# A fused attention and spectral filter kernel: two more key blocks moved off ScalarE, another closing sequence, and a new order of issue

## The chip, the cores and the metric

The kernel runs on one core of a Trainium2 chip. A core has five engines that work side by side and meet at semaphores: TensorE (matrix products, in the profile PE, its weight loads PEld), VectorE (DVE), ScalarE (ACT), GpSimd (POOL) and SyncE (SP), which here issues DMA transfers only. The working memory SBUF and the accumulators' memory PSUM have 128 partitions; TensorE writes only to PSUM, in banks of 512 float32 columns per partition. The metric is device time in microseconds; lower is better. The profile shows one execution, whose span runs from its first to its last instruction.

## The reference

Two branches over the same kind of input, mixed by a gate for each token. Branch A is multi-head attention over 2048 tokens with 16 heads of width 28. Branch B multiplies the two-dimensional Fourier transform of its input by a complex weight. (In this case both inputs are the same array, and the kernel reads it once.)

```python
g = sigmoid((x * gate_w).sum(-1, keepdims=True))      # x: 1 x 2048 x 448
qkv = (x @ wqkv) -> q, k, v of 16 heads, 28 wide
p = softmax(q @ k^T * 28**-0.5)                        # 16 x 2048 x 2048
a = (p @ v) @ wo
b = irfft2(rfft2(x) * (w_r + 1j * w_i))
return g * a + (1 - g) * b
```

## The kernel before

**Attention.** The heads are taken in four groups of four, the queries in four chunks of 512, so there are 16 rounds (group, chunk). A round goes over 16 key blocks of 128 keys. A unit is one head's product of a key block with a query chunk, 128 x 512 scores. Four heads lie in four row strips of TensorE, so that single scores of different heads can run beside each other. Per round and key block there is also a value product (`pv`): four column strips at once, the exponentials times the values, accumulated over all the round's blocks in one PSUM bank `pvb`. One more column of the values holds the weights alone, so that the bank also gets the softmax's denominators.

The exponential of a unit is taken in one of two ways, by key block:

- On ScalarE. Units follow each other in steps of three and two. A step's scores go to the PSUM slot `psA` (three banks) or `psB` (two banks), one ScalarE instruction (line 956) takes the exponentials of the whole slot into a ring in SBUF, and one value product per key block reads them.
- Off ScalarE. `ND` says how many of a round's blocks, counted from the last, go this way: 55 of 256. Each of the four units is one single score (`dunit`) into one of the two shared PSUM banks `bg`; VectorE adds an offset and writes the result as a 16-bit integer (`conv`, line 991), whose bits are read as a bfloat16 power of two with a linear mantissa. Three copies with integer offsets (`phase`, line 1002, 32, 64 and 96 steps) shift the mantissa's error, and four value products with scaled values `vd` add the four versions up, so that the errors average out. A block costs no ScalarE time, but four single scores, four conversions, three phase shifts and four value products instead of one. A phase shift runs on GpSimd, unless its number is in the list that ends `PLAN`; then it runs on VectorE (81 of 165).

**After a round** (`normalise`) VectorE copies the bank to SBUF (line 1070), a DMA gathers the denominators, VectorE takes the reciprocals, GpSimd multiplies them by the gate, two DMA stages spread them over the partitions (`Rb`), and GpSimd multiplies (line 1081). The last round (`last_norm`, from line 1091) does it without DMA: VectorE turns the bank in 32 x 32 blocks, takes reciprocals, multiplies by the gate, multiplies the values and turns back, all in two halves of 256 columns, one after the other.

**Branch B** is a chain of products with constant matrices through the same two `bg` banks, each evacuated by VectorE, with DMA regroupings between the stages.

**Output.** `out_tile` computes one of 16 blocks of 128 tokens by 448 in eight products: four for branch B, four for the four head groups. Blocks 12 to 15 need the last round: their eighth product is `late`. Blocks 12 and 13 are gathered in `bg` banks, 14 and 15 in the first banks of `psA` and `psB`, which are free behind the last exponentials. ScalarE copies three of them to SBUF and VectorE copies block 14, and the stores go out by SP (12, 14) and ScalarE's queue (13, 15).

**The gate** (`gate_item`, from line 876): ScalarE takes an exponential of 16 columns, four small VectorE operations (lines 880 to 885) follow, and a small product turns the result.

**The order.** Each of some 2,950 operations is recorded with its engine, inputs and a rough duration; a planner outside the kernel has put them in one order, packed as text in `PLAN` with the bank numbers and the list of phase shifts on VectorE. `issue` emits them in that order; an engine executes its own in order, so an instruction that waits holds up all behind it on its engine. `issue` adds one more kind of wait: when an operation of VectorE is marked `lk`, the next GpSimd operation in the order waits for it.

Of the kernel before, what the change touches and what calls it, by code (L numbers as in the profile page):

```python
# [16 lines left out]
ACT = mybir.ActivationFunctionType  # L17
# [14 lines left out]
ND = [0,3,3,4,4,4,4,4,4,4,4,4,4,4,3,2]  # L32
# [11 lines left out]
        'c-j@#V;dMovw-2*nOV$kY}>YN+qP}nwv#rt*@kUw+qRvw&3Vtq=MUW1gJ1x_LUa%yhy)5^fQQHsASOfshFA~*G(?5i&<)~14RBBi'  # L44
        '>Ox$o3H6{B#Dn?}A1Xp^XaEVI5j2N{&=@K}3upp~pd}=RrqBwKKpW@?Nue!7gig>7l0kdl8QMc~=mOE8gHH*mAT^|gjy?sXfnLxZ'
        'GD2lY2bmx}^oCBp2V{WE(AoEao{$ClLO<x@v%+A=26>^Y&ki|Y1muKVPznb7{E!dELT<<d1)wUFhS^XM3PDMj1BGEA6oF(o4$43Z'
        'Ope2#EX;*@P!x(mH7E}Ap#+qJ1+WmRz#=FQzrhwriCdw+p9H_dHrNiSaEPA_J0K0F#>FteFM*}74937)cn8a2pnnf(@dH$c6_5@;'
        '!W77WBOyJmgnoW1OoLT05vIcocrF<+6V8I2&>wceA21XCgrSfbv*2zR<WIvHI18&`5S)W-I0V+fdB}<vU;tc%OK=(1!82J8S0FoX'
        'fC;b>a^NV~40~Wa?1fFR4|3vg*bljIG#r3Dm>aLcUqJS6=nB{1Ivj+&cmvqpghP-I55rfu1^MwC+=c@93BJP}_yKjGAQr-(&;dTf'
        '7buKHup!)qW^fda!EyKpPQX1Vip6j(oPt$+AC7>rC!sZHyPAvR8ZLoZ{94ZHv-#}4B$mPzoWpw?>`ML@N@E%P4}JkCrBIc{a!BeC'  # L50
        'Jcjc41Xw+VbzA`-zzeW8f?dxQ@g-Eki1s;b=E_(FpTQ>H!ezX(Wqmnc-dDwHSiwiODb)t9j@!8grcyh2Bd1o8Y#LP)YhhZomBnu3'
        'sJ1pnvkze>*TE=u7r&HOQWxvtZceAttLQd^s*i8rwKTvOHlckZe{e?C5Z_88%xE*IM7A+D!9AQq?d6>6HRMvcRa0z+e{&v{)&9we'
        '?LlsiEpQ)au=_c)%A(TQn6@Rh!dGyBv#P&1n`(`1FuOX<hdI4H!%1yhJkISfi9Nxer9F1QBb>t~vtPujL+n&XJjq|B6N);;US+eL'
        'F{q>51#{YC96?1?U9lUU<47v98m_uy6x9PqsF5nAJ<Fq1Pwa)G)ius!d*gM!!hJA{y~=~sc^<4%*}iy*`{59EnTM+6wm)XJ!_);H'
        'fGO-nPHhL`AiTj*RdzcVhu|1BR*h5R)h!;1!!VkfprWgr977Gqv^J)?%Ofz2y~nZCNF0T^tX8pA9A#8=jH^cD7>uXxa}E1|AM#in'
        'hmZI+SFv|^Jig)y_?oNPr(DENR536nPQ*zV3n!`A7zc~m$ru+a*(V$ir(kg#Ulp@&cq&fA$*Q`2%a3`AnvNxGe4MIY@C>YK6X8pK'
        '#tCpH&cf%M1WVc?J|TYO+4zCy;3uwVYuVbisGp1Tu$X_(-=w&oj|=b}m+;@^ha^x5)lW&J7UClOM-r>jHi`NT|Ks1Wl>NoURZW{$'
# [160 lines left out]
class Op:  # L218
    def __init__(self, eng, dur, emit, deps, key, **a):
# [18 lines left out]
        self.id = None  # L238


class Item:
# [1113 lines left out]
```

## Time and profile before

| | |
|---|---|
| time, median of 3 runs | 393.71 us (393.5 to 394.0) |
| profiled execution, own time | 393.18 us |
| its span | 391.4 us |
| instructions | 11986 |
| PE busy | 375.8 us (96%) |
| ACT busy | 373.7 us (95%) |
| DVE busy | 325.6 us (83%) |
| POOL busy | 226.9 us (58%) |
| granted TensorE clock | 1.000 |

Busy time is the time in which at least one record of an engine runs. The records of ScalarE's and TensorE's neighbours overlap, so their pace is read from the distance of their starts. In a row of the view by order of time stand start, duration, engine, line, operation, output and inputs, shapes and, in brackets, the idle time before it with what ended it. In a row of the view by groups stand the count, the busy time, the mean duration in ns of one, and the group's idle time with what ended it. All matrix products carry the line of the helper that records them (415 or 423), so they are told apart by their tiles: `psA<-q,k` and `psB<-q,k` are scores for ScalarE, `bg<-q,k` single scores, `pvb<-ring,vw` and `pvb<-pd,vd` value products, `bg<-wo,q` and `bg<-Bd,X` output products.

### The profile page before, as it was taken

To read this page: it belongs to the slowest core of one execution; us is meant where nothing else is said; L and a number is where in the kernel's file an instruction comes from. 1 tells how busy PE (TensorE), PEld (TensorE's weight loads), DVE (VectorE), ACT (ScalarE), POOL (GpSimd) and SP (SyncE) were. 2 spreads that over 40 slices of the span, in tenths; PEclk is the share of its full clock that TensorE was granted. 3 is DMA by queue.
4 is the path that set the end of the run, shared out by engine and by line. 5 is a ranking of instruction groups with operands and counts; after the bars stand their busy time and mean duration, and the time that the engine had idled before them with its cause. 6 is when DMAs were issued, how large, how long until landed. Compare 5 with 4: busy or idle time off the path is not lost.

```text
span 391.4 us, 11986 instructions
## 1 busy us (share of the span) xinstructions
PE 375.8 (96%) x4926; PEld 139.0 (36%) x4926; DVE 325.6 (83%) x530; ACT 373.7 (95%) x340; POOL 226.9 (58%) x234
## 2 busy tenths in 40 slices
PE   8999999899999999999999999999999999999996
PEld 5643323234433334433333334422223332333332
DVE  2778777978799999999999999999999977977123
ACT  4999999899999999899999999999999999999993
POOL 7033777343965489868567786774655884524200
PEclk9999999999999999999999999999999999999999
DMA  8730000011202112222234122211012121010111
GB/s 208 175 107 3 3 13 2 4 17 32 88 10 67 42 28 72 65 74 58 49 91 130 27 66 66 66 39 39 3 38 93 61 72 43 22 62 26 53 37 60
DMA packets 31954, 21.64 MB, mean 55 GB/s; under 512 B 16716, under 2 KB 29740, under 8 KB 31900
## 3 DMA queue, kind: packets, MB, share of 16 engines
q1 hardware_dynamic: 30540, 20.43, 19.5%
q8 instruction: 38, 0.62, 0.6%
q10 hardware_dynamic: 1360, 0.46, 0.5%
q14 instruction: 16, 0.13, 0.1%
HBM read 15.00 MB, written 1.97 MB: 43 GB/s over the span
## 4 chain that ended last, share of the span: by engine, by line
PE 60%; DVE 19%; ACT 11%; issue 4%; DMA 3%; SPq 1%; POOL 1%; DVEq 0%; POOLq 0%; ACTq 0%
PE bg L415 28%; PE pvb L415 18%; ACT ring L956 10%; DVE pd L991 8%; PE psA L415 7%; PE psB L415 6%; DVE pd L1002 3%; DMA xtok<-in_A_x_dram 3%; SPq L398 1%; DVE tt L1244 1%; POOL pd L1002 1%; DVE pvs L1070 1%; PE bg L423 1%; DVE X L1193 1%; DVE k L721 1%
## 5 line engine op out<-in xcount | busy, mean ns | idle before, releaser
L956 ACT ACTIVATE ring<-psA 128x1536 bf16<-128x1536 f32 x157 | 233.5, 1487 | 2.6 <-PE psA L415 1.7
L1002 POOL TENSOR_SCALAR pd<-pd 128x2048 uint16<-128x2048 uint16 x84 | 159.3, 1903 | 61.5 <-DVE pd L1002 34.9
L956 ACT ACTIVATE ring<-psB 128x1024 bf16<-128x1024 f32 (+1 forms) x157 | 166.2, 1059 | 2.6 <-PE psB L415 2.5
L991 DVE TENSOR_SCALAR pd<-bg 128x512 uint16<-128x512 f32 x220 | 145.0, 683 | 12.6 <-PE bg L415 5.6
L415 PE MATMUL bg<-q,k 32*128 32x512 bf16 x220 | 81.1, 379 | 4.7 <-DVE pd L991 2.9
L415 PE MATMUL pvb<-pd,vd 128*32 128x512 bf16 x880 | 79.7, 384 | 0.7 <-DVE pd L1002 0.3
L415 PEld LDWEIGHTS <-k 32*128 32x128 bf16 x1024 | 37.0, 91 | 110.7 <-issue 105.8
L415 PE MATMUL pvb<-ring,vw 128*32 128x512 bf16 x784 | 74.0, 384 | 0.3 <-DVE pvs L1070 0.2
L415 PE MATMUL psA<-q,k 32*128 32x512 bf16 x483 | 65.0, 383 | 0.5 <-ACT ring L956 0.3
L415 PE MATMUL psB<-q,k 32*128 32x512 bf16 x321 | 64.1, 383 | 0.4 <-ACT pd L956 0.2
L1002 DVE TENSOR_SCALAR pd<-pd 128x2048 uint16<-128x2048 uint16 x81 | 58.2, 733 | 0.8
L415 PEld LDWEIGHTS <-vd 128*32 128x32 bf16 x880 | 21.1, 94 | 38.6 <-issue 33.9
L1081 POOL TENSOR_TENSOR q<-pvs,Rb 128x512 bf16<-128x512 f32 x15 | 19.1, 1271 | 24.9 <-DMA Rb<-rsc 21.0
L415 PEld LDWEIGHTS <-vw 128*32 128x32 bf16 x804 | 20.0, 95 | 30.1 <-issue 25.7
L415 PEld LDWEIGHTS <-xT 112*128 112x128 bf16 (+1 forms) x512 | 19.6, 97 | 10.9 <-issue 7.5
L1150 DVE CAST fin<-bg 128x448 bf16<-128x448 f32 x12 | 7.5, 622 | 19.2 <-PE bg L415 19.1
L869 POOL TENSOR_TENSOR vd<-vraw,wg 128x448 bf16<-128x448 f32 x16 | 14.9, 941 | 9.5 <-DVE pd L1002 7.7
L415 PE MATMUL bg<-xT,wpk 112*32 112x512 bf16 (+2 forms) x252 | 19.7, 377 | 0.5 <-POOL wpk L494 0.5
L415 PE MATMUL bg<-xT,wpq 112*32 112x512 bf16 (+1 forms) x240 | 18.4, 382 | 0.1
L1244 DVE TENSOR_TENSOR tt<-bg,Wg 128x900 bf16<-128x900 f32 x16 | 17.3, 1090 | 0.8 <-PE bg L415 0.4
L415 PE MATMUL bg<-wo,q 128*32 128x448 bf16 x224 | 17.4, 355 | 0.0
L415 PE MATMUL bg<-Bd,xT 112*32 112x450 bf16 x256 | 17.0, 356 | 0.0
(118 smaller groups left out, 326.5 us busy)
## 6 DMA issues: line engine op xcount, KB each, us to landing
Rb<-rsc SPq DMA_DIRECT2D x60, 64.0 KB
CS<-cCS SPq DMA_DIRECT2D x16, 192.0 KB
Wg<-in_B_w_i_dram SPq DMA_DIRECT2D x64, 28.1 KB
xtok<-Ab SPq DMA_DIRECT2D x16, 112.5 KB
V<-xtok SPq DMA_DIRECT2D x16, 112.5 KB
xtok<-in_A_x_dram SPq DMA_DIRECT2D x3, 448.0 KB
out_dram<-fin SPq DMA_DIRECT2D x12, 112.0 KB
Wg<-in_B_w_r_dram SPq DMA_DIRECT2D x32, 28.1 KB
```

The source lines that it names most:

```text
L398: self.pin(e.dma_start(out=out() if callable(out) else out, in_=in_() if callable(in_) else in_))
L415: self.pin(self.nc.tensor.matmul(out, lhsT=lhsT, rhs=rhs, start=start, stop=stop, **kw))
L423: self.pin(self.nc.tensor.transpose(out=out, in_=in_, identity=self.ident[0:n, 0:n]))
L721: self.pin(nc.vector.tensor_copy(out=dst, in_=self.bgi(it)))
L869: self.pin(nc.gpsimd.tensor_tensor(out=self.vd[g][:, f, :, :, 0:DH], in0=src, in1=wv, op=ALU.mult))
L956: self.pin(nc.scalar.activation(out=home[:, u0:u0 + len(st), :], in_=slot[:, 0:len(st), :], func=ACT.Exp, scale=LN2 / UNITS))
L991: self.pin(nc.vector.tensor_scalar(out=self.pd[y.bank][:, s, :].bitcast(U16), in0=self.bgi(it), scalar1=127 * UNITS, scalar2=0.0, op0=ALU. ...
L1002: self.pin(e.tensor_scalar(out=fl(self.pd[z.bank]), in0=fl(self.pd[y.bank]), scalar1=float(PHASE[f]), scalar2=1.0, op0=ALU.add, op1=ALU.mult))
L1070: ev = self.dve(0.6, lambda: self.pin(nc.vector.tensor_copy(out=pvs[:], in_=self.pv[:])), last + [self.nlast[i]], -1000.0, name="evac")
L1081: e = self.pool(1.24, lambda: self.pin(nc.gpsimd.tensor_tensor(out=dst, in0=pvs[:], in1=self.Rb[:], op=ALU.mult)), ds, kk)
L1150: e = self.dve(0.55, lambda: self.pin(nc.vector.tensor_copy(out=fin, in_=bank())), [ops[-1], self.fdma[t % 2]], key, **a)
L1244: self.pin(nc.vector.tensor_tensor(out=tt[:], in0=free_dims(self.bgi(it), [[0, 2], [F, 2], [1, F]]), in1=free_dims(Wg[:], [[F, 2], [F, 2], ...
```

## The change

- `ND` becomes 4 instead of 3 in rounds 2 and 14: 57 blocks off ScalarE. The units left are 796, in 319 steps; the last step is one unit in `psA`.
- The list of phase shifts on VectorE has 93 of now 171 entries.
- `last_norm` turns the bank in one piece of 512 columns, takes 16 reciprocals and 16 gate products at once, multiplies the first half of the columns on VectorE and the second on GpSimd, and turns both halves back on VectorE.
- Blocks 12, 13 and 15 gather in `bg` banks, 14 in `psA`. Of block 15 the first seven products are copied to SBUF in float32 (`vraw`) ahead of time; the eighth goes to the second bank of `psA` alone, and VectorE adds the two. VectorE copies block 13, ScalarE 12 and 14; ScalarE's queue stores block 14, SP the others.
- Three of the gate's VectorE operations are marked `lk`.
- The planner's figures for a value product (0.217 to 0.221) and for the DMA of `Rb` (2.3 to 2.8) are longer; they act only through the order.
- The order, the banks and the list are new.

```diff
-ND = [0,3,3,4,4,4,4,4,4,4,4,4,4,4,3,2]
+ND = [0,3,4,4,4,4,4,4,4,4,4,4,4,4,4,2]
 PLAN = (
...
         a = self.dve(0.12, lambda: self.pin(nc.vector.tensor_scalar(out=self.ge[:], in0=self.ge[:], scalar1=1.0,
-                                                                    scalar2=None, op0=ALU.add)), (e,), due)
+                                                                    scalar2=None, op0=ALU.add)), (e,), due, lk=True)
...
-                o = self.pe(0.217, fm, list(dict.fromkeys(deps)), k, mode="col", name="pv", pr=pr, grp=f"pv{n}")
+                o = self.pe(0.221, fm, list(dict.fromkeys(deps)), k, mode="col", name="pv", pr=pr, grp=f"pv{n}")
...
-                       (d2, self.rblast), kk, dur=0.46, lat=2.3, kb=64) for s in range(4)]
+                       (d2, self.rblast), kk, dur=0.46, lat=2.8, kb=64) for s in range(4)]
...
+        q = self.rrg[1]
+        tin = self.dve(0.62, lambda: self.pin(V.transpose(out=T[:], in_=self.pv[:])), last + [self.nlast[1]], K)
+        r = self.rr[1]
+        rc = self.dve(0.16, lambda: self.pin(V.reciprocal(out=r[:], in_=free_dims(T[:], [[32, 16]], DH))), (tin,), K + 2)
+        dv = self.dve(0.12, lambda: self.pin(V.tensor_tensor(out=q[:], in0=r[:], in1=free_dims(self.gbT[:], [[32, 16]]),
+                                                             op=ALU.mult)), (rc, self.gbt), K + 3)
+        tout = []
         for h in range(2):
+            def mul(h=h):
+                e = nc.gpsimd if h else V
+                self.pin(e.tensor_tensor(out=self.sq[:, 256 * h:256 * h + 256].rearrange("p (b j) -> p b j", j=32),
+                                         in0=T[:, 256 * h:256 * h + 256].rearrange("p (b j) -> p b j", j=32),
+                                         in1=free_dims(q[:], [[1, 8], [0, 32]], 8 * h), op=ALU.mult))
+            m = self.op("POOL" if h else "DVE", 0.7 if h else 0.38, mul, (dv,), K + 4 + h)
             cs = slice(256 * h, 256 * h + 256)
...
+            tout.append(self.dve(0.38, lambda cs=cs, h=h: self.pin(V.transpose(
+                out=self.q[3][:, 1536 + 256 * h:1792 + 256 * h], in_=self.sq[:, cs])), (m,), K + 6 + h))
...
-        it = Item() if i < 2 else None
-        bank = (lambda: self.bgi(it)[:, 0:D]) if it else (lambda: self.slots[i - 2][:, 0, 0:D])
+        it = None if t == 14 else Item()
+        bank = (lambda: self.bgi(it)[:, 0:D]) if it else (lambda: self.psA[:, 0, 0:D])
...
+        if t == 15:
+            e = self.dve(0.55, lambda: self.pin(V.tensor_copy(out=self.vraw[:], in_=bank())), ops[-1:] + self.vrawu,
+                         self.Tend - 4.0, **a)
+            last = self.psA[:, 1, 0:D]
+            m = self.pe(0.19, lambda: self.out_mm(t, 7, last, True, True), [late, self.lastexp[0]] + self.wod[3], -55.0,
+                        mode="col", name="late")
+            e = self.dve(0.55, lambda: self.pin(V.tensor_tensor(out=fin, in0=last, in1=self.vraw[:], op=ALU.add)), (m, e),
+                         key)
+        elif t == 13:
+            e = self.dve(0.55, lambda: self.pin(V.tensor_copy(out=fin, in_=bank())), ops[-1:], key, **a)
+        else:
             e = self.act(0.6, lambda: self.pin(nc.scalar.copy(out=fin, in_=bank())), ops[-1:], key, **a)
-        else:
-            e = self.dve(0.55, lambda: self.pin(nc.vector.tensor_copy(out=fin, in_=bank())), ops[-1:], key, **a)
-        self.dma(self.outv[:, t, :], fin, (e,), key, eng="ACT" if t % 2 else "SP")
+        self.dma(self.outv[:, t, :], fin, (e,), key, eng="ACT" if t == 14 else "SP")
```

More of the change, by code (lines that the diff above doesn't have):

```diff
@@ L1129, in out_tile @@
         i = t - 12
[L1130 to L1131 removed]
+        it = None if t == 14 else Item()
+        bank = (lambda: self.bgi(it)[:, 0:D]) if it else (lambda: self.psA[:, 0, 0:D])
         ops = []
[L1133 removed]
+        for k in range(7 if t == 15 else 8):
             def f(k=k):
[L1135 removed]
+                self.out_mm(t, k, bank(), k == 0, k == (6 if t == 15 else 7))
             d = ops[-1:]
@@ L1149, in out_tile @@
             fin = self.fin[t % 2][:]
-            e = self.dve(0.55, lambda: self.pin(nc.vector.tensor_copy(out=fin, in_=bank())), [ops[-1], self.fdma[t % 2]],
-                         key, **a)
+            e = self.dve(0.55, lambda: self.pin(V.tensor_copy(out=fin, in_=bank())), [ops[-1], self.fdma[t % 2]], key, **a)
             self.fdma[t % 2] = self.dma(self.outv[:, t, :], fin, (e,), key, dur=0.46, lat=2.8, kb=112)
```

163 lines of the change are left out of this document (73 added, 90 removed), and 19 rows, old and new, of the table PLAN.

## The prediction

> **What bounds the kernel now.** I read the page's busy line first, then the busy time stage by stage, then ScalarE's instructions in order of time, then the waits.
>
> ```profile
> PE 375.8 (96%) x4926; PEld 139.0 (36%) x4926; DVE 325.6 (83%) x530; ACT 373.7 (95%) x340; POOL 226.9 (58%) x234
> ...
> PE 60%; DVE 19%; ACT 11%; issue 4%; DMA 3%; SPq 1%; POOL 1%; DVEq 0%; POOLq 0%; ACTq 0%
> ```
>
> Two engines stand at 95 and 96% (first line), and the chain that ended last runs mostly over TensorE (second line). The table by stage (start:end, length, then busy time of each engine and its instruction count) says where each of them is full:
>
> ```profile
> core 0: us, PE busy (x) PEld busy (x) DVE busy (x) ACT busy (x) POOL busy (x), PEclk, DMA share, GB/s
> 12.00:80.00 68.00, 65.76 (x865) 24.34 (x867) 52.88 (x91) 66.00 (x63) 34.10 (x30) 1.00 0.17 43
> 80.00:120.00 40.00, 39.63 (x559) 15.08 (x551) 33.59 (x55) 39.95 (x38) 23.89 (x21) 1.00 0.11 34
> 120.00:200.00 80.00, 78.91 (x1071) 28.82 (x1063) 78.51 (x126) 78.33 (x70) 55.92 (x47) 1.00 0.25 63
> 200.00:300.00 100.00, 95.61 (x1216) 32.93 (x1205) 97.73 (x156) 99.98 (x90) 68.56 (x62) 1.00 0.21 55
> 300.00:360.00 60.00, 57.70 (x724) 19.90 (x724) 50.12 (x79) 59.14 (x53) 32.44 (x22) 1.00 0.17 50
> 360.00:383.00 23.00, 22.91 (x354) 8.26 (x348) 4.12 (x8) 22.37 (x21) 4.84 (x4) 1.00 0.16 49
> ```
>
> ScalarE lacks 5.2 us of 371 and is the first bound. TensorE lacks 10.5 us, but only 0.09 us from 360 on: there it is the bound. VectorE is full from 120 to 300 and has 15.1, 6.4, 9.9 and 18.9 us free in the other four stages; GpSimd is never full. The granted clock is 1.00 throughout.
>
> What ScalarE's time is made of, in rows of its instructions in order of time (start, duration) from two stretches:
>
> ```profile
> 9.85 1.45 ACT L956 ACTIVATE ring<-psA 128x1536 bf16<-128x1536 f32 x1 [0.63 <-PE psA L415]
> ...
> 371.52 1.45 ACT L956 ACTIVATE ring<-psA 128x1536 bf16<-128x1536 f32 x1
> 372.86 1.03 ACT L956 ACTIVATE ring<-psB 128x1024 bf16<-128x1024 f32 x1
> 373.76 1.47 ACT L956 ACTIVATE ring<-psA 128x1536 bf16<-128x1536 f32 x1
> ...
> 381.27 1.45 ACT L956 ACTIVATE ring<-psA 128x1536 bf16<-128x1536 f32 x1 [0.56 <-PE psB L415]
> 382.61 0.59 ACT L956 ACTIVATE ring<-psB 128x512 bf16<-128x512 f32 x1
> ```
>
> Records of neighbours overlap, so the price of an exponential is the distance of starts: 372.86 - 371.52 = 1.34 us for three units (a unit is one head's 128 keys by 512 queries) and 373.76 - 372.86 = 0.90 us for two. The program has 161 of the first, 160 of the second and the short one: 215.7 + 144.0 + 0.6 = 360.3 us, while they run from 9.85 to 383.20, 373.4 us. The 13 us between hold ScalarE's few small operations and, for the most part, waiting in small pieces. One wait is large:
>
> ```profile
> 71.68 1.90 POOL L1002 TENSOR_SCALAR pd<-pd 128x2048 uint16<-128x2048 uint16 x1 [3.95 <-PE psB L415]
> 72.03 1.58 DVE L880 TENSOR_SCALAR ge<-ge 128x16 f32<-128x16 f32 x1
> 74.36 0.23 PE L415 MATMUL bg<-ident,gg 128*32 128x128 bf16 x1 [1.35 <-DVE gg L884]
> 75.45 1.02 ACT L956 ACTIVATE ring<-psB 128x1024 bf16<-128x1024 f32 x1 [1.10 <-PE psB L415]
> ```
>
> A 16-column operation of the gate took 1.58 us on VectorE and ended at 73.61, with the GpSimd instruction beside it (73.58). TensorE stood 1.35 us at the gate's matmul, and the scores queued behind it came 1.10 us late.
>
> **The change, part by part. Two key blocks leave ScalarE** (rounds 2 and 14). That is 8 of 804 units: 796 are left, 159 pairs and one unit, so two instructions of three units and one of two go: 2 x 1.34 + 0.90 = 3.6 us off ScalarE. All of it counts if the other engines follow.
>
> What comes in its place, by these groups (busy us, mean ns):
>
> ```profile
> L1002 POOL TENSOR_SCALAR pd<-pd 128x2048 uint16<-128x2048 uint16 x84 | 159.3, 1903 | 61.5 <-DVE pd L1002 34.9 <-DVE pd L991 9.3 <-DVE sq L727 6.1
> L991 DVE TENSOR_SCALAR pd<-bg 128x512 uint16<-128x512 f32 x220 | 145.0, 683 | 12.6 <-PE bg L415 5.6 <-PE psB L415 4.3 <-PE psA L415 1.4
> L1002 DVE TENSOR_SCALAR pd<-pd 128x2048 uint16<-128x2048 uint16 x81 | 58.2, 733 | 0.8
> ```
>
> VectorE gets 8 conversions at 145.0 / 220 = 0.66 us, 5.3 us. Of 171 phase shifts (165 before) the list in the diff gives VectorE 93, not 81: 12 x 58.2 / 81 = 8.6 us. Together 13.9 us; GpSimd loses 6 x 1.9 = 11.4 us. Unpacked, the list puts 15 of VectorE's shifts into rounds 1 and 2, where it had 5, and round 2 also has four of the conversions: 10 x 0.72 + 4 x 0.66 = 9.8 us against 21.5 us free from 12 to 120. Round 14's four conversions (2.6 us) meet 9.9 us free. I take nothing for it. If that cover is gone, the conversions are late and TensorE waits (a rival below).
>
> TensorE, in rows of its order of time:
>
> ```profile
> 369.01 0.37 PE L415 MATMUL bg<-wo,q 128*32 128x448 bf16 x4
> 369.21 0.36 PE L415 MATMUL bg<-Bd,X 113*32 113x448 bf16 x4
> 369.41 0.39 PE L415 MATMUL pvb<-ring,vw 128*32 128x512 bf16 x4
> 369.63 0.56 PE L415 MATMUL bg<-Bd,X 113*32 113x448 bf16 x8
> 370.12 0.39 PE L415 MATMUL psB<-q,k 32*128 32x512 bf16 x2
> 370.43 0.37 PE L415 MATMUL bg<-wo,q 128*32 128x448 bf16 x4
> ```
>
> Four-part products start 0.20 to 0.22 us apart; a score step costs 0.31 us until the next product and about 0.1 more as it is entered (370.12, 0.29 after the second half of the x8). Six more value products are 6 x 0.22 = 1.3 us; three score steps less are -1.2 us. Eight more single scores cost between nothing (started beside a score step) and 0.31 each; I take the middle, 1.2 us. So +1.3 us in all, and its place decides. Unpacked, the new order has after the 22nd score step from the end 84 output products where the old one had 79, one value product more and one single score more: 5 x 0.19 + 0.22 + 0.2 = 1.4 us more work in the stage where TensorE lacks 0.09 us. That is **+1.4 us**. Ahead of that stage, ScalarE's time shrinks by 3.6 us while TensorE keeps about 1.9 us of the work done in it; TensorE has 10.4 us idle there, 1.35 of it the gate. Bounds: nothing, as in 200 to 300, where TensorE has 4.4 us idle and ScalarE still loses 0.02; or all 1.9. Nearer to the first: **+0.4 us**.
>
> The Trainium skill ("Perfetto Trace Analysis", Identifying the Most-Contended Engine) would judge TensorE's headroom by the share of weight loading, not by matmul time. That share is 36% here, and by it the sum would lose its +1.4 and +0.4; the starts 0.20 us apart with nothing between them speak against it for the last stage.
>
> **The gate.** Its three small operations now hold the next GpSimd instruction back until they end, and in the new order no phase shift is issued just ahead of them; its matmul also stands later behind its inputs. I take back the stall, between ScalarE's 1.10 and TensorE's 1.35: **-1.2 us**. Bounds: 0 (another GpSimd instruction is still running) and -1.35. The held GpSimd instruction has 33.9 us idle around it in its stage.
>
> **The end.** The last value bank before, VectorE in order of time:
>
> ```profile
> 383.74 0.45 DVE L1098 STREAM_TRANSPOSE pvs<-pvb 128x256 f32<-128x256 f32 x1 [2.86 <-PE pvb L415]
> 384.23 0.20 DVE L1102 RECIPROCAL rr<-pvs 128x8 f32<-128x8 f32 x1
> 384.47 0.17 DVE L1104 TENSOR_TENSOR rrg<-rr,gbT 128x8 f32<-128x8 f32 x1
> 384.67 0.42 DVE L1106 TENSOR_TENSOR sq<-pvs,rrg 128x256 bf16<-128x256 f32 x1
> 385.13 0.45 DVE L1112 STREAM_TRANSPOSE q<-sq 128x256 bf16<-128x256 bf16 x1
> ...
> 386.85 0.45 DVE L1112 STREAM_TRANSPOSE q<-sq 128x256 bf16<-128x256 bf16 x1
> 388.03 0.62 DVE L1158 CAST Ab<-psA 128x448 bf16<-128x448 f32 x1 [0.74 <-PE psA L415]
> ```
>
> From the bank's end to the second half's last turn: 383.74 to 387.30, 3.56 us. Rows for the new pieces:
>
> ```profile
> L1081 POOL TENSOR_TENSOR q<-pvs,Rb 128x512 bf16<-128x512 f32 x15 | 19.1, 1271 | 24.9 <-DMA Rb<-rsc 21.0 <-DVE pd L1002 3.9
> L1073 DVE RECIPROCAL rr<-rs 128x16 f32<-128x16 f32 x15 | 3.6, 242 | 0.7 <-DMA rs<-pvs 0.7
> L899 DVE STREAM_TRANSPOSE gbT<-gb 128x512 bf16<-128x512 bf16 x1 | 0.7, 701 | 0.0
> ```
>
> One turn of 512 columns 0.70, reciprocal 0.24, gate 0.20, half product 0.42 and two turns of 0.45, with 0.04 between: 2.6 us on VectorE. GpSimd's half takes 1.27 / 2 = 0.64 us beside the product and the first turn, so 0.1 late at most. The first half's turn ends at 2.2 us after the bank's end, where it ended at 1.84 before; the second at 2.6 to 2.7, not 3.56. But TensorE still has 20 products behind the bank, 20 x 0.19 = 3.8 us, some 21 before; it, not the turns, sets the end. Behind it VectorE adds block 15 (0.62) and then copies block 13 (0.62), and SP issues the store. I put that last issue 5.0 us after the last exponential; before it was 5.5 (388.65 from 383.20). **-0.4 us**; bounds +0.4 (one more 0.62 piece in the row of evacuations) and -0.9 (the whole gain of the turns). Three of the four stores are now SP's, one issue more on that queue, 0.6 us behind the one before. Block 14's early products can start only behind the last exponential, but 8 others stand ready around them.
>
> The Trainium skill ("SBUF — State Buffer", SBUF: two separate sides) says that a VectorE operation with two SBUF inputs and a GpSimd operation that reads SBUF exclude each other for the whole instruction. No row here shows that pair. By it GpSimd's half would start 0.42 us later and the second turn end at 2.9, which would take 0.2 off the gain at the end. The gate's stalled operation above agrees with such a lock.
>
> Block 15's early copy, 0.62 us more for VectorE, lies in the last stage, with 18.9 us free. The longer planning figures emit nothing; their effect is the order itself, in which SP's transfers move with the rounds they serve and keep their number.
>
> **Sum.** -3.6 + 1.4 + 0.4 - 1.2 - 0.4 = -3.4 us. The profiled execution took 393.18 us (span 391.4), 0.5 below the median 393.71; taken off the median: **390.3 us**.
>
> **Rivals.**
> 1. TensorE follows everywhere, also at the end: without the 1.4 and 0.4, 388.5 us. For it: TensorE lacks 10.5 us in all. Against: the row of 360 to 383.
> 2. The kernel is TensorE's throughout: ScalarE's 3.6 us only become waits, and 1.3 us of TensorE work come on top; the gate and the end remain: 393.7 + 1.3 - 1.2 - 0.4 = 393.4 us. The change then does not do what it says. For it: 60% of the chain that ended last is TensorE. Against: 200 to 300, where ScalarE never waits.
> 3. VectorE becomes the bound from 12 to 120. Every conversion frees one of the two shared PSUM banks, and TensorE works in order.
>
> ```profile
> PE bg L415 <- DVE pd L991: 3.6, 15, 0.3
> ```
>
> That wait is 0.24 us each, 15 times. The 20 added VectorE instructions, if each makes one product wait for a whole 0.66 us, give 13 us; at 0.24 us, 4.8 us. It decides from 0.17 us each (3.4 / 20). With 0.24 us each the time is 390.3 + 4.8 = 395.1 us. Against it: from 200 to 300 VectorE is 98% full and ScalarE is not held.
>
> **Numbers.** Chances: forecast 0.40 (389.3 to 391.8), first rival 0.24 (387.3 to 389.3), second 0.17 (391.8 to 394.2), third 0.19 (394.2 up). 0.2% is 0.8 us, about what a measurement of this kernel can tell from no change: below 392.9 lie the first two and some 0.06 of the second, 0.70; within 392.9 to 394.5 lies 0.11; above, 0.19. The range from 387.5 to 394.8 leaves out 0.03 below and 0.15 above.
>
> **What would show it.** Right: 319 exponentials, first start to last end near 369 us; no 1.5 us gate operation; VectorE about 90% busy from 12 to 120 with TensorE's waits on conversions under 8 us; TensorE without a gap behind 360, with ScalarE waiting 2 us or more there; last turn 2.7 us behind the bank's end. Wrong: ScalarE's idle time up by over 3 us ahead of 300 (second or third rival, told apart by whom TensorE waits for), or ScalarE free of waits behind 360 (first).

## The result, and the profile after

The changed kernel takes 389.75 us (median of 4 runs, 389.09 to 390.24), the kernel before 393.61 us beside it (393.32 to 394.00): ratio 0.990, 95% interval 0.9883 to 0.9918. The forecast was 390.3. The profiled execution took 389.7 us, its span fell from 391.4 to 387.9.

The page after, its busy line, its line of the chain that ended last and one of its groups:

```profile
PE 371.5 (96%) x4950; PEld 142.1 (37%) x4950; DVE 334.0 (86%) x548; ACT 369.0 (95%) x336; POOL 216.8 (56%) x229
...
PE 43%; DVE 23%; ACT 16%; issue 7%; DMA 5%; POOL 3%; SPq 2%; DVEq 0%; POOLq 0%; ACTq 0%
...
L1004 DVE TENSOR_SCALAR pd<-pd 128x2048 uint16<-128x2048 uint16 x93 | 64.4, 710 | 1.2
```

(The third line is VectorE's group of phase shifts: busy us, mean ns.) TensorE is 4.3 us less busy although it has 24 matmuls more; of the last chain it holds 43%, not 60%, and DMA has 5%. The table by stage (start:end, length, busy time of each engine with its instruction count):

```profile
12.00:80.00 68.00, 66.15 (x896) 25.88 (x895) 57.15 (x103) 65.96 (x63) 16.57 (x21) 1.00 0.19 46
80.00:120.00 40.00, 39.63 (x556) 15.14 (x552) 37.09 (x60) 39.45 (x36) 26.23 (x22) 1.00 0.15 39
120.00:200.00 80.00, 78.74 (x1061) 29.14 (x1057) 77.87 (x125) 79.08 (x72) 58.31 (x47) 1.00 0.24 56
200.00:300.00 100.00, 95.15 (x1225) 34.14 (x1225) 98.01 (x156) 99.87 (x90) 67.62 (x62) 1.00 0.25 58
300.00:360.00 60.00, 58.16 (x753) 20.80 (x745) 51.62 (x85) 59.77 (x53) 37.43 (x27) 1.00 0.16 47
360.00:380.00 20.00, 20.00 (x326) 8.06 (x328) 4.37 (x7) 18.02 (x17) 2.63 (x2) 1.00 0.20 56
```

VectorE (third figure) is at (57.15 + 37.09) / 108 = 87% from 12 to 120, TensorE has no gap from 360 to 380, and ScalarE stands 2.0 us there, 0.5 of them behind its last exponential. The changed kernel's instructions in order of time (start, duration; in brackets the wait before) at the head, at the gate and at the end:

```profile
10.24 1.45 ACT L957 ACTIVATE ring<-psA 128x1536 bf16<-128x1536 f32 x1 [0.70 <-PE psA L416]
...
18.54 1.10 PE L424 MATMUL bg<-ident,xtok 128*113 128x128 bf16 x16 [1.24 <-DMA xtok<-in_A_x_dram]
...
20.40 0.18 ACT L816 ACTIVATE w<-bg 128x16 f32<-128x16 bf16 x1 [1.40 <-PE bg L424]
...
70.48 0.17 DVE L881 TENSOR_SCALAR ge<-ge 128x16 f32<-128x16 f32 x1
...
75.79 1.90 POOL L1004 TENSOR_SCALAR pd<-pd 128x2048 uint16<-128x2048 uint16 x1 [14.47 <-DVE gT L891]
...
378.87 0.59 ACT L957 ACTIVATE ring<-psA 128x512 bf16<-128x512 f32 x1
380.15 0.72 DVE L1099 STREAM_TRANSPOSE pvs<-pvb 128x512 f32<-128x512 f32 x1 [0.70 <-PE pvb L416]
...
381.41 0.42 DVE L1108 TENSOR_TENSOR sq<-pvs,rrg 128x256 bf16<-128x256 f32 x1
381.46 0.86 POOL L1108 TENSOR_TENSOR sq<-pvs,rrg 128x256 bf16<-128x256 f32 x1 [15.92 <-DVE rrg L1102]
381.87 0.92 DVE L1113 STREAM_TRANSPOSE q<-sq 128x256 bf16<-128x256 bf16 x2
...
383.80 0.62 DVE L1162 TENSOR_TENSOR V<-psA,vraw 128x448 bf16<-128x448 f32 x1 [1.01 <-PE psA L416]
384.34 0.61 DVE L1165 CAST Ab<-bg 128x448 bf16<-128x448 f32 x1
...
384.46 0.53 ACT L1167 CAST Ab<-psA 128x448 bf16<-128x448 f32 x1 [1.13 <-DVE V L1162]
384.98 0.33 SPq L399 DMA_DIRECT2D out_dram<-Ab  x1
385.02 0.37 ACTq L399 DMA_DIRECT2D out_dram<-Ab  x1
```

What to see: the gate's operation takes 0.17 us, not 1.58, and no GpSimd instruction stands beside it. New is the head: TensorE waits 1.24 us for the last quarter of x, and ScalarE 1.40 behind it. At the end both stores go out at 385.0, 5.56 us behind the last exponential (379.46); before it was 5.48.

The accounts between the two profiles, by the distance of ScalarE's starts: what each step takes beyond 1.33 us (three units) or 0.903 us (two) is waiting or a small operation, added up over stretches of steps.

| part | before | after | difference | forecast |
|---|---|---|---|---|
| two exponentials of three units, one of two | | | -3.56 | -3.6 |
| start of the first exponential | 9.85 | 10.24 | +0.39 | 0 |
| steps 0 to 20 | 2.21 | 3.17 | +0.96 | 0 |
| steps 40 to 60 (the gate) | 1.92 | 0.68 | -1.24 | -1.2 |
| last 22 steps | 1.28 | 2.42 | +1.14 | +1.4 |
| all other steps | 8.75 | 7.31 | -1.44 | +0.4 |
| last exponential's end to the span's end | 8.18 | 8.46 | +0.28 | -0.4 |
| sum | | | -3.5 | -3.4 |

The sum came out near; several of its terms did not. One profile stands on each side, and the two rows ahead of step 20 scatter from execution to execution: over all the profiles below, the first exponential starts at 9.5 to 10.3 us whatever the order. The experiments go to the terms that missed, and to the claim under the first row, that ScalarE's time is what the kernel lacks.

### The profile page after: what moved, and what is told of

Same layout as the page of the kernel before. It is cut to its first block, busy times and chain, and to the rows that moved or that the text cites. A ratio compares the mean times of both kernels' runs of the same rounds, so it can differ in the third digit from the quotient of the medians.

```text
span 387.9 us, 12031 instructions
## 1 busy us (share of the span) xinstructions
PE 371.5 (96%) x4950; PEld 142.1 (37%) x4950; DVE 334.0 (86%) x548; ACT 369.0 (95%) x336; POOL 216.8 (56%) x229
## 4 chain that ended last, share of the span: by engine, by line
PE 43%; DVE 23%; ACT 16%; issue 7%; DMA 5%; POOL 3%; SPq 2%; DVEq 0%; POOLq 0%; ACTq 0%
PE bg L416 20%; ACT ring L957 16%; PE pvb L416 12%; DVE pd L992 10%; DVE pd L1004 5%; PE psA L416 5%; PE psB L416 5%; DMA xtok<-in_A_x_dram 3%; SPq L399 2%; DVE tt L1253 2%; POOL pd L1004 2%; DMA Rb<-rsc 1%; DMA rsc<-rrg 1%; DVE X L1296 1%; DVE pvs L1073 1%
## 5 line engine op out<-in xcount | busy, mean ns | idle before, releaser
L1004 POOL TENSOR_SCALAR pd<-pd 128x2048 uint16<-128x2048 uint16 x78 | 147.6, 1900 | 84.4 <-DVE pd L1004 31.7
L957 ACT ACTIVATE ring<-psB 128x1024 bf16<-128x1024 f32 x155 | 166.3, 1073 | 2.4 <-PE psB L416 2.3
L992 DVE TENSOR_SCALAR pd<-bg 128x512 uint16<-128x512 f32 x228 | 150.5, 683 | 10.1 <-PE bg L416 6.1
L416 PE MATMUL bg<-q,k 32*128 32x512 bf16 x228 | 84.6, 379 | 3.8 <-DVE pd L992 1.1
L416 PE MATMUL pvb<-pd,vd 128*32 128x512 bf16 x912 | 82.2, 384 | 1.2 <-DVE pvs L1073 0.5
L416 PEld LDWEIGHTS <-k 32*128 32x128 bf16 x1024 | 39.1, 91 | 111.7 <-issue 105.2
L416 PE MATMUL pvb<-ring,vw 128*32 128x512 bf16 x776 | 72.4, 384 | 0.3 <-POOL vw L818 0.3
L1004 DVE TENSOR_SCALAR pd<-pd 128x2048 uint16<-128x2048 uint16 x93 | 64.4, 710 | 1.2
L416 PE MATMUL bg<-xT,wpq 112*32 112x512 bf16 (+1 forms) x240 | 17.5, 382 | 0.2
L416 PE MATMUL bg<-Bd,X 113*32 113x448 bf16 x240 | 17.5, 355 | 0.0
```

The costliest lines, as they stand in the source:

```text
L416: self.pin(self.nc.tensor.matmul(out, lhsT=lhsT, rhs=rhs, start=start, stop=stop, **kw))
L957: self.pin(nc.scalar.activation(out=home[:, u0:u0 + len(st), :], in_=slot[:, 0:len(st), :], func=ACT.Exp, scale=LN2 / UNITS))
L992: self.pin(nc.vector.tensor_scalar(out=self.pd[y.bank][:, s, :].bitcast(U16), in0=self.bgi(it), scalar1=127 * UNITS, scalar2=0.0, op0=ALU. ...
L1004: self.pin(e.tensor_scalar(out=fl(self.pd[z.bank]), in0=fl(self.pd[y.bank]), scalar1=float(PHASE[f]), scalar2=1.0, op0=ALU.add, op1=ALU.mult))
```

## The experiments

Times are medians; the ratio is to the kernel before, run beside them on the same chip. Single runs of one kernel differ by several us (the kernel before: 393.45 to 399.29), and in the profiles most of such a difference lies ahead of step 20, so the verdicts go by stretches of steps of the profiled execution: us between the starts of exponentials, the last column to the end of the last one. (Steps 260 to 307, left out, take 53.5 to 54.3 us, in pv_drop 55.7, 2 us of them at steps 296 to 299; what varies there is told below, under the last 22 steps.)

| kernel | time | ratio, 95% interval | 0-20 | 20-60 | 60-200 | 200-260 | 307-315 | 315-end |
|---|---|---|---|---|---|---|---|---|
| after | 389.75 | 0.990 (0.9883 to 0.9918) | 25.50 | 45.72 | 161.59 | 67.82 | 10.15 | 4.42 |
| tail_psB | 389.32 | 0.9879 (0.9853 to 0.9904) | 25.66 | 45.74 | 161.63 | 67.83 | 10.15 | 4.42 |
| two_halves | 390.32 | 0.9921 (0.9891 to 0.9952) | 25.78 | 45.72 | 161.64 | 67.82 | 10.13 | 4.42 |
| gp_alone | 388.54 (one) | | 24.46 | 45.72 | 161.59 | 67.85 | 10.15 | 4.42 |
| x3_early | 388.12 | 0.9851 (0.9832 to 0.9870) | 25.26 | 45.72 | 161.64 | 67.95 | 10.15 | 4.42 |
| both | 387.91 | 0.9842 (0.9825 to 0.9858) | 24.25 | 45.72 | 161.63 | 67.82 | 10.15 | 4.42 |
| exp_mid | 390.79 | 0.9881 (0.9841 to 0.9921) | 25.44 | 45.75 | 161.63 | 67.79 | 10.15 | 4.42 |
| pv_drop | 391.65 | 0.9921 (0.9894 to 0.9948) | 27.00 | 45.73 | 161.63 | 67.67 | 10.15 | 4.42 |
| mid_both | 388.43 | 0.9838 (0.9786 to 0.9889) | 26.17 | 45.74 | 161.59 | 66.81 | 10.13 | 4.42 |
| exp_end | 389.78 | 0.9879 (0.9831 to 0.9927) | 25.38 | 45.72 | 161.64 | 67.80 | 10.15 | 4.42 |
| out_drop | 389.13 | 0.9851 (0.9820 to 0.9882) | 25.31 | 45.72 | 161.63 | 67.80 | 9.32 | 4.73 |
| shifts_short | 388.87 | 0.9831 (0.9772 to 0.9890) | 28.69 | 45.70 | 161.35 | 67.82 | 10.13 | 4.42 |

In the columns behind step 20 the untouched stretches agree within 0.2 us, so a difference of 0.3 there can be read from one profile.

### The end: which wait is last?

**The last product in another slot.** Block 15's late product goes to `psB`, not to the second bank of `psA`, whose first bank holds block 14:

```diff
-            last = self.psA[:, 1, 0:D]
-            m = self.pe(0.19, lambda: self.out_mm(t, 7, last, True, True), [late, self.lastexp[0]] + ...
+            last = self.psB[:, 0, 0:D]
+            m = self.pe(0.19, lambda: self.out_mm(t, 7, last, True, True), [late, self.lastexp[1]] + ...
```

> The changed kernel with one edit: block 15's late product goes to the first bank of psB, not to the second of psA. Theory: in the changed kernel VectorE's addition waited for block 14's late product in psA (its row of waits names psA; 383.80 against 383.31, where its own product ended) and ScalarE's copy of block 14 waited for that addition, because both use the tile psA. With tiles of their own the addition starts near 0.4 us sooner, ScalarE's copy 0.7 us sooner, the last store is issued 0.3 to 0.4 us sooner: 389.4 us against 389.75. Rival: the evacuations stand behind TensorE's last product anyway: 389.75, no change.

Its last turns in order of time:

```profile
379.71 0.72 DVE L1099 STREAM_TRANSPOSE pvs<-pvb 128x512 f32<-128x512 f32 x1 [0.70 <-PE pvb L416]
...
382.98 0.62 DVE L1162 TENSOR_TENSOR V<-psB,vraw 128x448 bf16<-128x448 f32 x1 [0.63 <-PE psB L416]
383.31 0.53 ACT L1167 CAST Ab<-psA 128x448 bf16<-128x448 f32 x1 [0.41 <-PE psA L416]
...
384.17 0.33 SPq L399 DMA_DIRECT2D out_dram<-Ab  x1
```

The addition starts 3.27 us behind the bank, not 3.65 (383.80 - 380.15), ScalarE's copy no longer waits for it, and the last issue is 5.15 us behind the last exponential (379.02): 0.41 less. In the changed kernel VectorE waited for block 14's product and ScalarE for VectorE, although no data passed between them: the waits go by the tile `psA`, not by its banks.

**The old closing sequence in the new order.** The bank is turned in two halves, one after the other, all on VectorE:

```diff
-        tin = self.dve(0.62, lambda: self.pin(V.transpose(out=T[:], in_=self.pv[:])), last + [self.nlast[1]], K)
...
+        def second():
+            for fn in (turn, recip, gate, mul, back):
+                fn(1)
...
+        t0 = self.dve(0.38, lambda: back(0), (m0,), K + 6)
+        t1 = self.dve(0.38, second, (m1,), K + 7)
```

> The changed kernel with the last value bank turned as before: two halves of 256 columns on VectorE one after the other, GpSimd without a part. All else as changed. The second turn back then ends 3.56 us behind the bank (row of before), not 2.64 as in the changed kernel, and block 15's late product, which started 2.80 us behind the bank's turn, waits for it: 0.8 us later, 390.5 us, if the turns set the end. If TensorE's queue of 20 products alone sets it, as the prediction had it, under 0.3 us more: 390.0 us or less.

```profile
379.52 0.45 DVE L1101 STREAM_TRANSPOSE pvs<-pvb 128x256 f32<-128x256 f32 x1 [0.70 <-PE pvb L416]
...
382.62 0.45 DVE L1116 STREAM_TRANSPOSE q<-sq 128x256 bf16<-128x256 bf16 x1
...
383.98 0.62 DVE L1176 TENSOR_TENSOR V<-psA,vraw 128x448 bf16<-128x448 f32 x1 [0.91 <-PE psA L416]
```

The last turn ends 3.55 us behind the start of the bank's first (0.91 later than 2.64), the addition starts 4.46 behind it (0.81 later than 3.65), the last issue 6.37 us behind the last exponential (0.81 later than 5.56). So with the old turns the end waits for them, and in this order the new sequence is worth 0.81 us. TensorE's last products in the changed kernel, then in this one, say where:

```profile
381.92 1.01 PE L416 MATMUL bg<-wo,q 128*32 128x448 bf16 x16
382.76 0.55 PE L416 MATMUL psA<-wo,q 128*32 128x448 bf16 x8
```

```profile
381.29 0.95 PE L416 MATMUL bg<-wo,q 128*32 128x448 bf16 x16
382.05 0.38 PE L416 MATMUL psA<-wo,q 128*32 128x448 bf16 x4
383.12 0.37 PE L416 MATMUL psA<-wo,q 128*32 128x448 bf16 x4 [0.69 <-DVE q L1116]
```

Four four-part products take 0.76 us here (381.29 to 382.05), then TensorE does one more and stands for the last turn. In the changed kernel four take 0.84 (381.92 to 382.76), and the 0.08 us more are all that TensorE loses to the turns behind the bank: there its row of 20 products, and not the turns, sets the pace up to the last product.

**GpSimd alone.** Both halves of the product on GpSimd, none on VectorE:

```diff
             def mul(h=h):
-                e = nc.gpsimd if h else V
-                self.pin(e.tensor_tensor(out=self.sq[:, 256 * h:256 * h + 256]...
+                for j in ((0, 1) if h == 0 else ()):
+                    self.pin(nc.gpsimd.tensor_tensor(out=self.sq[:, 256 * j:256 * j + 256]...
```

> The changed kernel, but GpSimd does both halves of the last product, one after the other, and VectorE none; nothing is left out. The first half then has no VectorE operation beside it. If its 0.86 us in the changed kernel came from the VectorE product beside it (two inputs from SBUF, in the Trainium skill's "SBUF — State Buffer", SBUF: two separate sides, such a pair excludes each other): the first half takes 0.64 to 0.70 us. If it is GpSimd's own price for 256 columns in this form: 0.86 again. The second half runs beside the first turn. The second turn ends some 3.2 to 3.5 us behind the bank instead of 2.64, and the last store is issued 0.4 to 0.8 us later behind the last exponential than 5.56.

The rows of that kernel's last product and turns in order of time:

```profile
378.74 0.72 DVE L1099 STREAM_TRANSPOSE pvs<-pvb 128x512 f32<-128x512 f32 x1 [0.70 <-PE pvb L416]
...
380.04 1.19 POOL L1108 TENSOR_TENSOR sq<-pvs,rrg 128x256 bf16<-128x256 f32 x2 [15.47 <-DVE rrg L1102]
380.69 1.02 DVE L1114 STREAM_TRANSPOSE q<-sq 128x256 bf16<-128x256 bf16 x2 [0.73 <-POOL sq L1108]
```

Each half takes 0.616 us, the second one too, beside VectorE's turn, which has one input. So the 0.86 us of the changed kernel came from the VectorE product beside it. The turns end 2.97 us behind the bank, the last issue 5.80 us behind the last exponential (378.05): 0.24 later than in the changed kernel, less than expected. The short time of this run is its head (24.46).

### The head: the last quarter of x

**x earlier.** The transfer of x's last quarter is put on SP ahead of three transfers of branch B's weights:

```diff
+        order.remove(x3)
+        order.insert(order.index(first), x3)
```

> The changed kernel with one edit: the transfer of the last quarter of x is issued ahead of three spectral-weight transfers on SP's queue, about 1.2 us sooner than at 13.85 us. Theory: TensorE's wait of 1.24 us at 17.3 to 18.5 us for this transfer, new in the changed kernel, is all lost time, since ScalarE stood 1.4 us behind it: 388.6 us. Rival: the next stage of the same start (projections, weights' transfers, the exponentials of the key weights) is late as well, and little comes back: 389.4 us or more.

```profile
17.59 1.10 PE L430 MATMUL bg<-ident,xtok 128*113 128x128 bf16 x16 [0.32 <-DMA xtok<-in_A_x_dram]
...
19.45 0.18 ACT L822 ACTIVATE w<-bg 128x16 f32<-128x16 bf16 x1 [0.48 <-PE bg L430]
```

ScalarE's wait there falls from 1.40 to 0.48 us; steps 0 to 20 fall by 0.24 only, in one profile each. The medians speak more plainly: 388.12 us (387.59 to 389.03), with an interval of the ratio that lies below that of the changed kernel. The wait is lost time, then.

**Both edits.** x early and the late product in `psB`:

> Both edits together. If the two losses are separate, the gains add up: 388.3 us. If the first is eaten up by the stages behind it, 389.3 us.

387.91 us (387.61 to 387.95; before beside it 394.04): 1.6% below the kernel before, the lowest median of all and the steadiest. ScalarE has no wait over 0.4 us between its first exponential and 36 us, and steps 0 to 20 take 24.25 us. Over the ten profiles with the changed kernel's head TensorE's wait for x at this place is 0.20 us once (gp_alone) and 1.05 to 1.91 us otherwise; in two profiles with the old head it is 0.20 and 0.98. In those ten profiles SP issues that transfer at 13.3 to 14.7 us, in the two of the old head at 12.9 and 13.3. But where x arrives alike, the two orders take the same: with a wait of 0.20 us steps 0 to 20 take 24.46 us in the new order and 24.54 in the old, with 1.05 (out_drop) and 0.98 (before_gate) they take 25.31 and 25.30. So the late x costs the changed kernel time, and the edit brings it back; how much of that loss the old order has too is open, with two profiles of it and no run of it with x early.

### Who sets the pace

**Less ScalarE in the middle.** Four exponentials of steps 220 to 232 work on one unit instead of three:

```diff
+                w = 1 if self.unit_step[st[0]] in (220, 224, 228, 232) else len(st)
-                self.pin(nc.scalar.activation(out=home[:, u0:u0 + len(st), :], in_=slot[:, 0:len(st), :],
+                self.pin(nc.scalar.activation(out=home[:, u0:u0 + w, :], in_=slot[:, 0:w, :],
```

> The changed kernel with four of ScalarE's three-unit exponentials in the middle (steps 220, 224, 228, 232) cut to one unit; the other two units of each read what an earlier step left, so the output isn't the reference's. That takes 4 x 0.86 = 3.4 us off ScalarE and nothing off any other engine. If ScalarE is the bound there and TensorE can follow, as the prediction has it for the stages ahead of 360 us: 386.4 to 387.5 us. If TensorE or VectorE is the bound (second rival): 389 us or more.

**Less TensorE in the middle.** Seven value products of round 10 are left out:

```diff
+                    if kind == "d" and n == 10 and f in (1, 2) and not a and not z and (kt, f) != (12, 2):
+                        return
```

> The changed kernel without seven value products of round 10 (the second and third versions of its off-ScalarE blocks, so that the output lacks them). 7 x 0.22 = 1.5 us less for TensorE in the middle, where ScalarE is held to be the bound: 389.3 to 389.8 us, next to nothing gained. If TensorE is the bound throughout (second rival): 388.2 us.

**Less ScalarE and less VectorE.** The cut of exp_mid, and VectorE's phase shifts of rounds 10 to 12 on 8 columns:

```diff
+                    w = 8 if e is nc.vector and n in (10, 11, 12) else 2048
-                    self.pin(e.tensor_scalar(out=fl(self.pd[z.bank]), in0=fl(self.pd[y.bank]), ...
+                    self.pin(e.tensor_scalar(out=fl(self.pd[z.bank])[:, 0:w], in0=fl(self.pd[y.bank])[:, 0:w], ...
```

> The changed kernel with four exponentials of steps 220 to 232 cut from three units to one (3.4 us off ScalarE, as in exp_mid) and VectorE's phase shifts of rounds 10 to 12 cut to 8 columns (14 or so, some 9 us off VectorE); eight units' exponentials and most of those shifted copies are not computed. exp_mid gained nothing in the steps 200 to 260 (67.8 us). If VectorE was what held them there: steps 200 to 260 now fall by 2 to 3.4 us or more, to 64.4 to 66, and VectorE shows gaps between 255 and 290. If TensorE holds them, or the planned order does through something else: they stay within 0.5 us of 67.8, and TensorE shows no gaps there.

The stretch from 255 to 290 us, busy times in the order PE, PEld, DVE, ACT, POOL, in the changed kernel, in exp_mid and in mid_both:

```profile
255.00:290.00 35.00, 32.45 (x405) 10.32 (x401) 34.47 (x57) 35.00 (x32) 22.87 (x23) 1.00 0.21 52
```

```profile
255.00:290.00 35.00, 32.41 (x406) 10.36 (x405) 34.45 (x57) 32.49 (x33) 22.82 (x23) 1.00 0.20 56
```

```profile
255.00:290.00 35.00, 32.71 (x413) 10.17 (x409) 27.74 (x59) 33.13 (x33) 23.60 (x23) 1.00 0.22 58
```

exp_mid takes the time off ScalarE (35.00 to 32.49) and off nothing else: steps 200 to 260 take 67.79 us, as before the cut, and VectorE stays full. Seven value products less (1.5 us of TensorE) leave 67.67. (The long time of pv_drop, 391.65, lies in its head, 27.00, and in steps 260 to 307.) With VectorE relieved too they take 66.81: 1.0 us gained of the 3.4. The longest wait of VectorE in mid_both from 255 to 285 us (engine, line and what it waited for: us, times, longest) is:

```profile
DVE pd L993 <- PE bg L416: 3.2, 5, 1.2
```

Now VectorE waits for TensorE's single scores, while TensorE is busy 32.71 us of 35: no engine is full, and what holds the rest, TensorE or the order, isn't told apart. So from 200 to 300 us ScalarE and VectorE are full together, and time taken off ScalarE alone buys nothing. That VectorE comes first is not shown: no run took time off it alone, and by the prices 60 steps of ScalarE take 30 x (1.33 + 0.903) = 66.99 us, so of 67.82 at most 0.8 could come back.

**Less ScalarE at the end.** The same cut in steps 300, 304, 308 and 312:

> The same cut of 3.4 us of ScalarE's time, but in steps 300, 304, 308 and 312, behind 356 us; the output isn't the reference's. If TensorE is the bound there, as the prediction has it: under 1 us gained, 388.8 to 389.7 us. If ScalarE is still the bound (first rival): 386.4 us.

**Less TensorE at the end.** Seven of branch B's and the head groups' output products of blocks 8 to 11 are left out, in steps 308 to 314:

```diff
+                if (t, k) in ((8, 2), (8, 3), (9, 2), (9, 3), (10, 4), (10, 5), (11, 3)):
+                    return
```

> The changed kernel without seven of the 512 column-strip output products' quadruples (blocks 8 to 11, issued between score steps 308 and 314); blocks 8 to 11 of the output lack these terms. 7 x 0.19 = 1.3 us less for TensorE in its last stage and nothing less for ScalarE. If TensorE is the bound there: 1.0 to 1.3 us gained, 388.5 to 388.8 us. If ScalarE is: 389.7 us, no change.

The stretch from 356 to 378 us (columns as above) in the changed kernel, exp_end and out_drop:

```profile
356.00:378.00 22.00, 22.00 (x346) 8.15 (x339) 5.59 (x10) 20.57 (x19) 5.22 (x4) 1.00 0.19 51
```

```profile
356.00:378.00 22.00, 22.00 (x346) 8.32 (x347) 5.22 (x9) 17.90 (x19) 5.23 (x4) 1.00 0.17 51
```

```profile
356.00:378.00 22.00, 21.49 (x330) 7.95 (x330) 5.35 (x10) 21.06 (x19) 5.22 (x4) 1.00 0.15 47
```

ScalarE's 2.7 us less buy nothing: TensorE is busy 22.00 of 22.00 and steps 307 to the end take 14.57 us in both, and from step 300 on, with all four cuts, it is 22.69 and 22.68. Seven products less, 7 x 0.19 = 1.3 us of TensorE, make steps 307 to 315 0.83 us shorter, of which 0.31 come back behind 315. The net gain is 0.52 us, half of the least that was expected for TensorE as the bound, and where ScalarE was the bound it would be nothing; together with exp_end this says that TensorE sets the pace here, as the prediction had it.

**Less VectorE at the front.** VectorE's 13 phase shifts of rounds 2 and 3 on 8 columns, with the edit of mid_both for other rounds:

> The changed kernel, but VectorE's 13 phase shifts of rounds 2 and 3 work on 8 columns instead of 2048, so most of these shifted copies are not computed. That takes some 8 us off VectorE between 50 and 120 us. Theory of the prediction (the added VectorE work of rounds 1 to 3 lies beside other work, taken as free): steps 20 to 60 stay at 45.7 us and 60 to 200 at 161.6, the time at 389.7, within 0.5. Third rival (VectorE holds the shared banks and so TensorE there): the time falls by 2 us or more, most of it in steps 20 to 80.

Steps 20 to 60 take 45.70 us (45.72), 60 to 200 161.35 (161.59): 0.26 us, while VectorE is busy 6.3 us less (334.0 to 327.7). The third rival falls, as far as rounds 2 and 3 go; round 1, which also got shifts on VectorE, was left as it is. The long head of this profile, like that of pv_drop, had a lower granted clock; its row from 10 to 36 us shows 0.87:

```profile
10.00:36.00 26.00, 24.14 (x291) 13.39 (x290) 15.49 (x29) 20.90 (x22) 4.16 (x10) 0.87 0.46 108
```

### The gate

**The gate's part alone.** The kernel before, with the three operations marked and the one phase shift behind them:

```diff
-                                                                    scalar2=None, op0=ALU.add)), (e,), due)
+                                                                    scalar2=None, op0=ALU.add)), (e,), due, lk=True)
...
+        order.remove(shift.id)
+        order.insert(order.index(gate[3].id) + 1, shift.id)
```

> The kernel before with one part of the change alone: the gate's three small VectorE operations are marked lk, and the one phase shift that stood on GpSimd just ahead of them is issued behind them. Nothing is left out. If the stall at the gate was lost time (term of -1.2 us): the 1.5 us operation of the gate becomes one of about 0.1 us, TensorE's 1.35 us at the gate's matmul go, and the time falls by 1.1 to 1.35 us against the kernel before, to about 392.5. Rival, that the pace of the next steps takes the stall up again (VectorE or GpSimd late by the shift that was moved): the stall goes from the rows, and the time changes by less than 0.4 us.

It takes 394.96 us (393.35 to 396.8), ratio 1.0003 (0.9971 to 1.0035): no gain. Its rows in order of time:

```profile
72.81 0.17 DVE L886 TENSOR_SCALAR ge<-ge 128x16 f32<-128x16 f32 x1
...
73.87 1.90 POOL L1008 TENSOR_SCALAR pd<-pd 128x2048 uint16<-128x2048 uint16 x1 [5.33 <-DVE gg L890]
...
74.21 2.10 DVE L1008 TENSOR_SCALAR pd<-pd 128x2048 uint16<-128x2048 uint16 x1
...
78.09 0.37 PE L421 MATMUL bg<-q,k 32*128 32x512 bf16 x1 [1.51 <-DVE pd L997]
```

The gate is quick (0.17 us), but the moved GpSimd shift now stands beside a VectorE shift, which takes 2.10 us instead of 0.68 and ends 0.54 us behind it (76.31 and 75.77); the VectorE instructions behind are late, and TensorE waits 1.51 us for a conversion. Steps 40 to 60 take 24.24 us, 24.25 in the kernel before: the stall has moved by some 4 us. What the gate lost is the price of a GpSimd and a VectorE instruction that exclude each other; in the changed kernel it is gone, and there the order leaves GpSimd idle from 61.3 to 75.8 us.

## The prediction, step by step

- **Two key blocks off ScalarE, -3.6.** Count and size came as worked out: 319 exponentials in 369.2 us. The reason given, that ScalarE is the first bound, does not hold where it was tried: cutting 3.4 us of ScalarE alone bought nothing in steps 200 to 260 and nothing behind step 300. ScalarE's 99.9% did not mean that the others had time left: VectorE was 98% busy in the same stage. But neither cut lies in rounds 2 and 14, which the two blocks left and where VectorE had time. That the change gains may be due to the blocks, or to the new order as a whole (TensorE 4.3 us less busy, ScalarE 4.7, the held shifts below); no run has the new order with the old `ND`, so this is not shown.
- **VectorE's additions, free.** Right: 0.26 us for 6.3 us (shifts_short), and TensorE's matmuls wait less for conversions than before (3.6 us):

```profile
PE bg L416 <- DVE pd L992: 2.1, 9, 0.4
```

VectorE became 8.4 us busier, not 13.9: the shifts' mean fell from 733 to 710 ns, and the gate's operation by 1.4 us.
- **TensorE in the last 22 steps, +1.4.** The mechanism is right, and both tests of the stage agree; the size is half luck. Of the +1.14, 0.4 us lie in steps 298 and 299, where TensorE stands 0.35 us for a GpSimd shift (354.91). That wait changes with the execution: gp_alone and two_halves have none, pv_drop 1.3 us. Without it the last 22 steps wait 1.91 us, 0.63 more than before, and the forecast 1.4 is over twice that. The Trainium skill's rule cited in the prediction ("Perfetto Trace Analysis", Identifying the Most-Contended Engine) would have misled by the weight loads' share alone: it is 8.15 / 22 = 37%, and TensorE is the bound. The section names the matmuls' share of peak FLOPs (MFU) beside it, which neither the prediction nor a row here worked out.
- **TensorE ahead of that, +0.4.** Wrong in sign: -1.44. (The upper bound of 1.9 us that the prediction gave for this term is not worked out there.) Part of it is a size: by the starts of TensorE's products, a score step with a single score beside it takes on average 0.04 to 0.11 us longer than one without (before: two units 330 and 401 ns, three 324 and 437; after: 330 and 374, 364 and 427; waits included), not 0.15, and runs of scores fell from 311 to 306, 134.7 to 129.9 us. The other part is VectorE: shifts that GpSimd held beyond 0.9 us were 7 before, 3.5 us in all, and are 4 now, 1.2 us; three of the 7, 2.0 us, lay from 327 to 346 us, and 1.14 of the 1.44 us were gained in the 38 steps ahead of the last 22, around it. Those steps vary by 0.4 us between executions of the new order. No run took the two parts apart; this stays open.
- **The gate, -1.2.** The size is right in steps 40 to 60 (-1.24). The prediction named the marks and the new order together. before_gate shows that the marks with one shift moved bring nothing; in the changed kernel no GpSimd instruction takes the place of the one held back. The prediction's bound of 0 is what before_gate measured, though by another way than it gave: not an instruction still running, but the moved one, which met the next VectorE shift.
- **The end, -0.4.** Wrong: +0.08 on the last issue. The second turn ended 2.64 us behind the bank, as forecast (2.6 to 2.7), and "TensorE, not the turns, sets the end" held: the turns cost TensorE 0.08 us behind the bank, where the old ones would have cost 0.8 more (two_halves). The step that failed is what stands behind TensorE. The prediction's pieces in a row (bank 0.54, products 3.8, addition and copy 0.62 each) make 5.6 us; its 5.0, which it does not work out, needs the addition to start while TensorE's last products still run. In the changed kernel the addition waited for block 14's product, the last but one, since both lie in one tile `psA`: 0.41 us (tail_psB). Another 0.15 is the bank, which came 0.69 us behind the last exponential (380.15 - 379.46), 0.54 before. Without these two the last issue would stand at 5.56 - 0.41 - 0.15 = 5.0 us, the forecast.
- **GpSimd's half, 0.64.** Its own price is 0.616, and 0.86 beside VectorE's product. The Trainium skill ("SBUF — State Buffer", SBUF: two separate sides) has the two exclude each other for the whole instruction, and the trace agrees: VectorE's product ends at 381.84, GpSimd's 0.48 us behind it, so all but its first 0.14 us waited. It cost nothing, since VectorE's first turn ended at the same time (382.3); the 0.2 us that the prediction would have taken off by that rule were not lost.
- **In no term: the head, +1.35.** The first exponential came 0.39 us later, within the scatter of 9.5 to 10.3, and the first 20 steps took 0.96 more, with TensorE waiting 1.24 us for x's last quarter instead of 0.20. The prediction counted that transfer as moved with its round and priced it at nothing. That x comes late in the changed kernel is a loss (x3_early); that the new order makes it one is not shown, since the profile before is one with an early x.

**The rivals.** The first (TensorE follows everywhere) falls by exp_end and out_drop. The second (TensorE's throughout) falls as a time and by pv_drop, where 1.5 us less of TensorE in the middle gave 0.15. The third falls by shifts_short. The forecast's nearness is partly luck: +1.35 at the head and +0.5 to 0.7 at the end that were not seen, against -1.84 ahead of the last 22 steps that was not seen either. By the medians the time fell by 3.9 us, 389.75 from 393.61.

## What to carry to other kernels

A busy share near 100% names a candidate, not the bound: where several engines are within a few per cent, cut the candidate's work in one stage and look at the distance of the steps, since a relief of one engine alone may buy nothing. When an order is made anew, check the arrival of each early transfer against its first use, in several executions, and the waits that a shared tile makes between data that have nothing to do with each other; the two edits that came from this, one transfer earlier and one product in another tile, brought the ratio from 0.990 (0.9883 to 0.9918) to 0.9842 (0.9825 to 0.9858). A stall between GpSimd and VectorE isn't removed by moving the GpSimd instruction next to another VectorE instruction of the same kind.

## What the runs showed of the hardware

- In the profiles of before, after and before_gate, 19 VectorE phase shifts (128 x 2048, 0.68 us alone) took over 0.9 us. Each had started while a GpSimd instruction was running, and every one ended 0.543 to 0.549 us behind that instruction's end, whatever it had waited (0.36 to 1.55 us). That is a lock for the whole instruction, and only the first 0.14 us of the waiting instruction go beside the other. The product on GpSimd shows the same 0.14 us from the other side.
- A VectorE turn (one input) beside a GpSimd product costs neither anything: 0.446 and 0.616 us, as alone.
- From step 20 to step 200 the profiles of eleven kernels with the new order (all but shifts_short) take 207.31 to 207.38 us; where their executions differ without an edit, it is mostly in the first 36 us and, by up to 2 us, between steps 260 and 307.
